# Early chunks transposed on TensorE, input loads gated behind the weights, and both matmul phases in sequence, in a retention and gated MLP kernel on one core

## The chip, the core and the metric

The kernel runs on one core of one Trainium2 chip. Times are device microseconds of that core. The kernel before took 371.13 us (median of three runs, 371.1 to 371.18). "Ratio" below always means the ratio of a kernel's fast runs to the fast runs of the kernel before in the same rounds, on the same chip ("fast": not over 1.5% above the fastest run of that kernel). It is not quite the ratio of the medians that stand beside it.

Engine names: PE is TensorE (matmul), PEld its weight load, DVE is VectorE, ACT is ScalarE, POOL is GpSimd, SP is SyncE, whose queue issues the input loads. "ACTq" and "SPq" are the issuing queues. Times inside a trace count from the start of the profiled span. PSUM is the memory that the matmuls here write to; a buffer of it can be used again only when another engine has copied the result out. A semaphore is a counter that instructions wait on; each DMA here raises one when it has completed.

## The reference

```python
# q, k, v: (8 batches, 8 heads, 576 positions, 64); float32
scores = (1/8) * q @ k.T
ret    = scores * gamma[h] ** (i - j)   for i >= j, else 0
attn   = ret @ v
x      = attn as (4608 tokens, 512)          # tokens = batch x position
h      = x @ w_in                            # 512 -> 2048
out    = (h * cos(h)) @ w_out                # 2048 -> 512, float32
```

## The kernel before

Attention works in chunks of up to 128 positions, five to a batch (128, 128, 128, 128, 64), with a running state per batch. A "full chunk" is one of 128 rows; a batch is 4.5 of them. Each chunk is loaded (q, k, v), scaled to bf16 (`qs`, `ks`, `vb`), and q and k are transposed by the DMA. The MLP works on nine tiles of 512 tokens: `mm1` gives h and g = h cos(h) for one of 16 slices of the 2048 columns, `mm2` projects back.

```python
def prep(b, c, eng_k, eng_v):                # scale to bf16, then transpose by DMA
    ...
    for dst, src in ((qT, qs), (kT, ks)):
        nc.sync.dma_start(dst[:, :, :sz], src[:sz]..., transpose=True)

def mm1(t, et):                              # h = x w_in, one of 16 slices
    ps = ps_mm.tile([P, 512], F32, tag="mm") # one of FOUR PSUM buffers, shared with mm2
    ... 4 matmuls into ps
    nc.scalar.activation(cosh, ps, Sin, bias=half_pi)
    nc.vector.tensor_mul(gT[:, et, :], ps, cosh)

def mm2(t, s):                               # o = g w_out, four matmuls a call
    ... accumulate into ps (the same four buffers)
    if qt == 3:
        nc.scalar.copy(ot, ps)               # ScalarE empties PSUM ...
        nc.scalar.dma_start(out[...], ot)    # ... and its queue issues the store

# start: loads of batch 0, preps, w_in; loads of batch 1; attention of batch 0;
# preps of batch 1, w_out, loads of batch 2; then
for t in range(NT + 1):
    for s in range(16):
        if s % 3 == 0 and s // 3 < 5:
            prep(t + 2, s // 3, ...); load(t + 3, s // 3)
        mm1(t, s); mm2(t - 1, s)             # the two phases interleaved, a tile apart
        ... one unit of the attention of batch t + 1
```

## Time and profile before

| | before |
|---|---|
| median time | 371.13 us |
| profiled span | 367.2 us |
| TensorE busy, 0 to 104 us | 47 us |
| TensorE busy, 138 to 171 us | 33 of 33 us |

The page divides the span into 40 slices (9.2 us each). A digit is the busy share in tenths, PEclk the granted TensorE clock, DMA the share of the DMA engines. Before:

```profile
PE   0013708683899999999999999999999999999995
...
PEclk9999999898799999999999999999999999999999
DMA  9999999999999999998997999721000011001012
```

TensorE works in bursts with gaps for the first eleven slices (47 of 104 us) and is full from then on. The DMA row is full for the first half. So the kernel has two stages, and only the first can be shortened without taking work from TensorE. Busy time by stretches of the span (columns: stretch, its length, then PE, PEld, DVE, ACT and POOL busy us with instruction counts, granted clock, DMA share, GB/s), before:

```profile
0.00:50.00 50.00, 11.38 (x116) 6.70 (x116) 16.05 (x35) 6.79 (x10) 17.02 (x25) 1.00 1.18 191
50.00:104.00 54.00, 35.86 (x250) 16.60 (x251) 27.83 (x39) 14.41 (x22) 27.09 (x32) 0.91 1.19 191
...
138.00:171.00 33.00, 33.00 (x239) 15.87 (x238) 21.20 (x30) 13.11 (x20) 14.80 (x17) 1.00 1.10 207
```

What TensorE waits for in the first stage, from the view of the waits (total us, times, longest), before:

```profile
PE sc L122 <- DMA kT<-ks: 55.5, 8, 20.8
```

Scores wait for the DMA transposes of k; the longest wait is 20.8 us. Two lines of TensorE's timeline (start, length, instruction, and in brackets the idle time just before and who ended it), then one of POOL's, all of the kernel before:

```profile
56.64 0.60 PE L122 MATMUL sc<-qT,kT 64*128 64x128 bf16 x8 [12.32 <-DMA kT<-ks]
...
84.48 1.03 PE L228 MATMUL o<-w_out_sb,gT 128*128 128x512 bf16 x4
```

```profile
56.85 3.04 POOL L278 DMA_DIRECT2D w_out_sb<-in_moe_w_out_dram  x4
```

w_out is issued only at 56.85 us, and the first output-projection matmul runs at 84.48 us.

### The profile page before, as it was taken

How to read it: one execution, taken by the hardware profiler on the slowest of the kernel's cores; microseconds unless marked ns; L12 is line 12 of the kernel's file. 1: busy time of each engine (PE TensorE's matmuls, PEld its weight loads, DVE VectorE, ACT ScalarE, POOL GpSimd, SP SyncE). 2: the span in 40 equal slices, each digit the busy share in tenths (PEclk: the TensorE clock that was granted, in tenths of full speed). 3: DMA queues.
4: the chain of work that ended last, by engine and by line, in shares of the span. 5: the costliest groups of instructions: out<-in, count | busy, mean ns of one | idle time of the engine just before them, and what ended most of it. 6: DMA issues, size and time to landing. Idle time of an engine off the chain costs nothing.

```text
span 367.2 us, 5413 instructions
## 1 busy us (share of the span) xinstructions
PE 306.3 (83%) x2048; PEld 145.7 (40%) x2048; DVE 187.6 (51%) x276; ACT 126.1 (34%) x189; POOL 104.9 (29%) x125
## 2 busy tenths in 40 slices
PE   0013708683899999999999999999999999999995
PEld 0002403241344444544544444445444444444442
DVE  2223605592567477556656664766576534334300
ACT  2220002242233434334334333443433354454421
POOL 3240475057544454452651524320000000000000
PEclk9999999898799999999999999999999999999999
DMA  9999999999999999998997999721000011001012
GB/s 173 209 152 199 208 202 143 198 207 202 206 180 186 213 202 206 191 231 185 192 210 167 188 203 198 172 73 43 30 29 30 30 41 46 31 37 49 30 62 81
DMA packets 161370, 51.75 MB, mean 141 GB/s; under 512 B 152640, under 2 KB 156736, under 8 KB 161344
## 3 DMA queue, kind: packets, MB, share of 16 engines
q1 hardware_dynamic: 151936, 37.77, 60.6%
q0 software_dynamic: 4224, 4.19, 7.3%
q10 hardware_dynamic: 5184, 9.44, 7.3%
q8 instruction: 16, 0.26, 0.3%
q14 instruction: 10, 0.08, 0.1%
HBM read 36.70 MB, written 9.44 MB: 126 GB/s over the span
## 4 chain that ended last, share of the span: by engine, by line
PE 72%; DMA 13%; SPq 11%; POOL 2%; issue 1%; DVE 1%; ACT 0%; POOLq 0%
PE o L228 32%; PE h L209 31%; SPq L88 8%; DMA kT<-ks 7%; DMA fq<-in_q_dram 3%; DMA fv<-in_v_dram 3%; PE sc L122 3%; PE ov L179 3%; SPq L110 2%; PE st L144 1%; PE ov L169 1%; POOL qs L101 1%; POOL vb L106 1%; DVE ret L130 0%; ACT cosh L217 0%
## 5 line engine op out<-in xcount | busy, mean ns | idle before, releaser
L217 ACT ACTIVATE cosh<-h,half_pi 128x512 f32<-128x512 f32 x144 | 98.8, 687 | 205.2 <-PE h L209 203.0
L218 DVE TENSOR_TENSOR gT<-h,cosh 128x512 bf16<-128x512 f32 x144 | 99.5, 691 | 113.8 <-ACT cosh L217 113.1
L209 PE MATMUL h<-xT,w_in_sb 128*128 128x512 bf16 x576 | 152.8, 389 | 0.0
L228 PE MATMUL o<-w_out_sb,gT 128*128 128x512 bf16 x576 | 145.5, 380 | 0.0
L228 PEld LDWEIGHTS <-gT 128*128 128x128 bf16 x576 | 56.5, 98 | 68.4 <-issue 0.8
L209 PEld LDWEIGHTS <-w_in_sb 128*128 128x128 bf16 x576 | 50.1, 99 | 52.8 <-issue 3.8
L101 POOL TENSOR_TENSOR qs<-fq,gq 128x512 bf16<-128x512 f32 (+1 forms) x40 | 41.7, 1042 | 77.9 <-DMA fq<-in_q_dram 77.5
L122 PE MATMUL sc<-qT,kT 64*128 64x128 bf16 (+1 forms) x320 | 16.8, 231 | 55.6 <-DMA kT<-ks 55.5
L130 DVE TENSOR_TENSOR ret<-sc,tri 128x1024 bf16<-128x1024 f32 (+1 forms) x40 | 44.3, 1108 | 32.0 <-PE sc L122 31.9
L102 POOL TENSOR_TENSOR ks<-fk,gk 128x512 bf16<-128x512 f32 (+1 forms) x35 | 36.5, 1042 | 23.6 <-DMA kT<-ks 16.6
L122 PEld LDWEIGHTS <-kT 64*128 64x128 bf16 (+1 forms) x320 | 9.7, 103 | 72.5 <-DMA kT<-ks 59.6
L106 POOL CAST vb<-fv 128x512 bf16<-128x512 f32 (+1 forms) x35 | 21.3, 610 | 41.9 <-PE ov L179 34.9
L237 ACT COPY ot<-o 128x512 f32<-128x512 f32 x36 | 21.1, 586 | 17.1 <-PE o L228 16.9
L188 DVE CAST xT<-ov 128x512 bf16<-128x512 f32 (+1 forms) x40 | 25.3, 633 | 1.3 <-PE ov L179 0.8
L153 DVE TENSOR_TENSOR sb<-st,diag_104 128x512 bf16<-128x512 f32 x32 | 21.8, 681 | 0.0
L179 PE MATMUL ov<-ret,vb 128*64 128x128 bf16 (+1 forms) x320 | 17.0, 232 | 0.0
L169 PE MATMUL ov<-qT,sb 128*128 128x128 bf16 (+1 forms) x128 | 12.5, 225 | 1.4 <-DVE xT L188 1.4
L144 PE MATMUL st<-vb,ks 128*128 128x128 bf16 x128 | 13.5, 233 | 0.0
L169 PEld LDWEIGHTS <-sb 128*128 128x128 bf16 x128 | 9.8, 103 | 9.1 <-issue 2.8
L144 PEld LDWEIGHTS <-ks 128*128 128x128 bf16 x128 | 10.2, 104 | 7.7 <-issue 1.5
L179 PEld LDWEIGHTS <-vb 128*64 128x64 bf16 (+1 forms) x320 | 10.5, 116 | 6.5 <-issue 3.9
L102 DVE TENSOR_TENSOR ks<-fk,gk 128x512 bf16<-128x512 f32 (+1 forms) x5 | 3.6, 715 | 14.3 <-DMA fk<-in_k_dram 14.3
(22 smaller groups left out, 14.7 us busy)
## 6 DMA issues: line engine op xcount, KB each, us to landing
out_dram<-ot ACTq DMA_DIRECT2D x36, 256.0 KB, 2.1
fq<-in_q_dram SPq DMA_DIRECT2D x32, 256.0 KB, 4.3
fk<-in_k_dram SPq DMA_DIRECT2D x32, 256.0 KB, 4.6
fv<-in_v_dram SPq DMA_DIRECT2D x32, 256.0 KB, 5.1
w_in_sb<-in_moe_w_in_dram POOLq DMA_DIRECT2D x4, 512.0 KB, 10.5
w_out_sb<-in_moe_w_out_dram POOLq DMA_DIRECT2D x4, 512.0 KB, 10.8
fq<-in_q_dram SPq DMA_DIRECT2D x8, 128.0 KB, 3.9
fk<-in_k_dram SPq DMA_DIRECT2D x8, 128.0 KB, 4.5
```

The costliest lines, as they stand in the source:

```text
L88: nc.sync.dma_start(f[:sz], src[b, :, c * P : c * P + sz, :].rearrange("h s d -> s h d"))
L101: nc.gpsimd.tensor_tensor(out=qs[:sz], in0=fq[:sz], in1=tq, op=ALU.mult)
L102: eng_k.tensor_tensor(out=ks[:sz], in0=fk[:sz], in1=tk, op=ALU.mult)
L122: nc.tensor.matmul(ps[:sz, he, hg, :sz], lhsT=kT[d0 : d0 + D, hg, :sz], rhs=qT[d0 : d0 + D, hg, :sz], start=True, stop=True,)
L130: nc.vector.tensor_tensor(out=ret[:sz, :, :, :sz].rearrange("p a b i -> p (a b) i"), in0=ps[:sz, :, :, :sz].rearrange("p a b i -> p (a b) i"),
L144: nc.tensor.matmul(ps[:, hg, :], lhsT=ks[:, 2 * hg : 2 * hg + 2, :].rearrange("s h d -> s (h d)"), rhs=vb[:, 2 * hg : 2 * hg + 2, :].rearr ...
L169: nc.tensor.matmul(ps[:, hg, :sz], lhsT=sb[:, hg, :], rhs=qT[:, hg, :sz], start=(hg == 0), stop=False, skip_group_check=True,)
L179: nc.tensor.matmul(ps[he * D : he * D + D, hg, :sz], lhsT=vb[:sz, 2 * hg + he, :], rhs=ret[:sz, he, hg, :sz], start=(c == 0 and hg == 0), ...
L209: nc.tensor.matmul(ps, lhsT=w_in_sb[:, dg, et * P : (et + 1) * P], rhs=xT[:, dg, t0 : t0 + T_TILE], start=(dg == 0), stop=(dg == DG - 1),)
L217: nc.scalar.activation(cosh, ps, ACTF.Sin, bias=half_pi, scale=1.0)
L218: nc.vector.tensor_mul(gT[:, et, :], ps, cosh)
L228: nc.tensor.matmul(ps, lhsT=gT[:, et, tsi * P : (tsi + 1) * P], rhs=w_out_sb[:, et, :], start=(et == 0), stop=(et == ET - 1),)
```

## The change

The intent is to make the start short. Chunks 0 to 7 are transposed on TensorE instead of by DMA. Loads of chunks 4, 5 and 6 (and, as the queue is in order, all later ones) wait until parts of w_out have landed. The first tiles have 512, 256 and 256 tokens, so that less attention has to be ready for tiles 1 and 2. Each tile does all of mm1, then all of mm2, with the attention of the next tile between the mm2 matmuls. In tile 0 the mm2 of its four 128-token groups advances side by side; later tiles finish one `o` after the other. The core of the diff (cuts marked):

```diff
+    widths = [512, 256, 256] + [512] * 7
+    N_PE_T = 8
+    AHEAD = 6
+    LEAD = 4
+    GATED = {4: 4, 5: 6, 6: 7}
-    op = ctx.enter_context(tc.tile_pool(name="op", bufs=3))
+    op = ctx.enter_context(tc.tile_pool(name="op", bufs=4))
 ...
+        if g >= N_PE_T:
+            for m in range(2):
+                nc.sync.dma_start(qkT[:, m, :, :sz], ..., transpose=True)
 ...
+    def transposes(g):                        # chunks 0..7
+        ps = ps_ov.tile([P, 2, HG, P], BF16, tag="ov", name="tr")
+        ... 8 x nc.tensor.transpose(ps[...], qks[...], ident)
+        nc.vector.tensor_copy(qkT[:, :, :, :sz], ps[:, :, :, :sz])
+
+    def scores(g):
+        if g >= 4:
+            feed(g + 1 + LEAD)                # loads up to AHEAD chunks further, then preps
 ...
+    for g in range(4):
+        prep(g, nc.vector, nc.scalar)
+        if g == 2: load_w_in(0, 256); load_w_in(256, 512)
+    ... rest of w_in, then w_out in four parts
+    for u in units(0, 4): u()
 ...
+    for n, w in enumerate(widths):
+        for et in range(ET):
+            mm1(n, et)
+        ...
+        for i, group in enumerate(groups):    # groups of four mm2 matmuls
+            for tsi, et in group:
+                mm2(n, tsi, et)               # ends, as before, with nc.scalar.copy(ot, ps)
+                                              # and nc.scalar.dma_start(out[...], ot)
+            ... the next tile's attention units, spread over the groups
```

More of the change, by code (lines that the diff above doesn't have):

```diff
@@ L44 @@
     gammas = [1.0 - 2.0 ** (-5.0 - h) for h in range(H)]
-    T_TILE = 512
-    NT = NTOK // T_TILE
     DG = DM // P
     ET = DF // P
-    NQ = T_TILE // P
+    widths = [512, 256, 256] + [512] * 7
+    assert sum(widths) == NTOK
+    starts = [sum(widths[:n]) for n in range(len(widths))]
+    chunks = [(b, c) for b in range(B) for c in range(NC)]
+    N_PE_T = 8
+    AHEAD = 6
+    LEAD = 4
+    GATED = {4: 4, 5: 6, 6: 7}
     consts = ctx.enter_context(tc.tile_pool(name="consts", bufs=1))
@@ L64 @@
     ps_mm = ctx.enter_context(tc.tile_pool(name="ps_mm", bufs=4, space=bass.MemoryType.PSUM))
-    order = ctx.enter_context(tc.manual_schedule())
+    ctx.enter_context(tc.manual_schedule())
     pos_i = consts.tile([P, NC, H], I32)
@@ L77 @@
     diag2 = consts.tile([P, P], F32)
+    ident = consts.tile([P, P], BF16)
     w_in_sb = consts.tile([P, DG, DF], BF16)
@@ L82, with load, prep @@
     tiles = {}
-    def load(b, c):
+    def load(g):
+        b, c = chunks[g]
         sz = csz[c]
+        first = None
         for name, src in (("q", q), ("k", k), ("v", v)):
             f = ld.tile([P, H, D], F32, tag="f" + name, name=f"f{name}")
-            nc.sync.dma_start(
+            i = nc.sync.dma_start(
                 f[:sz], src[b, :, c * P : c * P + sz, :].rearrange("h s d -> s h d")
             )
-            tiles["f" + name, b, c] = f
-    def prep(b, c, eng_k, eng_v):
+            first = first or i
+            tiles["f" + name, g] = f
+        return first
+    def prep(g, eng_k, eng_v):
+        b, c = chunks[g]
         sz = csz[c]
-        fq, fk, fv = (tiles.pop(("f" + n, b, c)) for n in "qkv")
-        qs = nat.tile([P, H, D], BF16, tag="qs", name="qs")
-        ks = nat.tile([P, H, D], BF16, tag="ks", name="ks")
+        fq, fk, fv = (tiles.pop(("f" + n, g)) for n in "qkv")
+        qks = nat.tile([P, 2, H, D], BF16, tag="qks", name="qks")
         vb = nat.tile([P, H, D], BF16, tag="vb", name="vb")
@@ L100, in prep @@
         tk = gk[:sz, c, :].unsqueeze(2).to_broadcast([sz, H, D])
-        nc.gpsimd.tensor_tensor(out=qs[:sz], in0=fq[:sz], in1=tq, op=ALU.mult)
-        eng_k.tensor_tensor(out=ks[:sz], in0=fk[:sz], in1=tk, op=ALU.mult)
+        nc.gpsimd.tensor_tensor(out=qks[:sz, 0], in0=fq[:sz], in1=tq, op=ALU.mult)
+        eng_k.tensor_tensor(out=qks[:sz, 1], in0=fk[:sz], in1=tk, op=ALU.mult)
         if eng_v is nc.scalar:
@@ L106, in prep @@
             eng_v.tensor_copy(vb[:sz], fv[:sz])
-        kT = trp.tile([P, HG, P], BF16, tag="kT", name="kT")
-        qT = trp.tile([P, HG, P], BF16, tag="qT", name="qT")
-        for dst, src in ((qT, qs), (kT, ks)):
-            nc.sync.dma_start(
-                dst[:, :, :sz], src[:sz].rearrange("s h d -> s (h d)"), transpose=True
-            )
-        tiles["a", b, c] = (ks, vb, qT, kT)
-    def scores(b, c):
-        sz = csz[c]
-        ks, vb, qT, kT = tiles["a", b, c]
+        qkT = trp.tile([P, 2, HG, P], BF16, tag="qkT", name="qkT")
+        if g >= N_PE_T:
+            for m in range(2):
+                nc.sync.dma_start(
+                    qkT[:, m, :, :sz],
+                    qks[:sz, m].rearrange("s h d -> s (h d)"),
+                    transpose=True,
+                )
+        tiles["a", g] = (qks, vb, qkT)
+    def transposes(g):
+        sz = csz[chunks[g][1]]
+        qks, vb, qkT = tiles["a", g]
+        ps = ps_ov.tile([P, 2, HG, P], BF16, tag="ov", name="tr")
+        for m in range(2):
+            for hg in range(HG):
+                nc.tensor.transpose(
+                    ps[:, m, hg, :sz],
+                    qks[:sz, m, 2 * hg : 2 * hg + 2, :].rearrange("s h d -> s (h d)"),
+                    ident[:sz, :sz],
+                )
+        nc.vector.tensor_copy(qkT[:, :, :, :sz], ps[:, :, :, :sz])
+    def scores(g):
+        if g >= 4:
+            feed(g + 1 + LEAD)
+        sz = csz[chunks[g][1]]
+        qks, vb, qkT = tiles["a", g]
         ps = ps_sc.tile([P, 2, HG, P], F32, tag="sc", name="sc")
@@ L123, in scores @@
                     ps[:sz, he, hg, :sz],
-                    lhsT=kT[d0 : d0 + D, hg, :sz],
-                    rhs=qT[d0 : d0 + D, hg, :sz],
+                    lhsT=qkT[d0 : d0 + D, 1, hg, :sz],
+                    rhs=qkT[d0 : d0 + D, 0, hg, :sz],
                     start=True,
@@ L135, in scores, with state @@
         )
-        tiles["ret", b, c] = ret
-    def state(b, c):
-        ks, vb, qT, kT = tiles["a", b, c]
+        tiles["ret", g] = ret
+    def state(g):
+        b, c = chunks[g]
+        qks, vb, qkT = tiles["a", g]
         if c == 0:
@@ L145, in state @@
                 ps[:, hg, :],
-                lhsT=ks[:, 2 * hg : 2 * hg + 2, :].rearrange("s h d -> s (h d)"),
+                lhsT=qks[:, 1, 2 * hg : 2 * hg + 2, :].rearrange("s h d -> s (h d)"),
                 rhs=vb[:, 2 * hg : 2 * hg + 2, :].rearrange("s h d -> s (h d)"),
@@ L158, in state, with attn_out @@
         )
-        tiles["sb", b, c + 1] = sb
-    def attn_out(b, c):
+        tiles["sb", g + 1] = sb
+    def attn_out(g):
+        b, c = chunks[g]
         sz = csz[c]
-        ks, vb, qT, kT = tiles.pop(("a", b, c))
-        ret = tiles.pop(("ret", b, c))
+        qks, vb, qkT = tiles.pop(("a", g))
+        ret = tiles.pop(("ret", g))
         ps = ps_ov.tile([P, HG, P], F32, tag="ov", name="ov")
         if c > 0:
-            sb = tiles.pop(("sb", b, c))
+            sb = tiles.pop(("sb", g))
             for hg in range(HG):
@@ L171, in attn_out @@
                     lhsT=sb[:, hg, :],
-                    rhs=qT[:, hg, :sz],
+                    rhs=qkT[:, 0, hg, :sz],
                     start=(hg == 0),
@@ L188, in attn_out, with units, mm1 @@
         nc.vector.tensor_copy(xT[:, :, t0 : t0 + sz], ps[:, :, :sz])
-    def attention_units(b):
-        u = [
-            lambda: scores(b, 0), lambda: state(b, 0), lambda: scores(b, 1),
-            lambda: attn_out(b, 0), lambda: state(b, 1), lambda: scores(b, 2),
-            lambda: attn_out(b, 1), lambda: state(b, 2), lambda: scores(b, 3),
-            lambda: attn_out(b, 2), lambda: state(b, 3), lambda: scores(b, 4),
-            lambda: attn_out(b, 3), lambda: attn_out(b, 4),
-        ]
-        return u
-    def mm1(t, et):
-        t0 = t * T_TILE
+    def units(g0, g1):
+        u = []
+        if g0 < min(g1, N_PE_T):
+            u.append(lambda g=g0: transposes(g))
+        for g in range(g0, g1):
+            if g + 1 < min(g1, N_PE_T):
+                u.append(lambda g=g + 1: transposes(g))
+            u.append(lambda g=g: scores(g))
+            if g > g0:
+                u.append(lambda g=g - 1: attn_out(g))
+            if chunks[g][1] < NC - 1:
+                u.append(lambda g=g: state(g))
+        if g1 > g0:
+            u.append(lambda g=g1 - 1: attn_out(g))
+        return u
+    def mm1(n, et):
+        t0, w = starts[n], widths[n]
         if et == 0:
-            tiles["g", t] = gp.tile([P, ET, T_TILE], BF16, tag="gT", name="gT")
-        gT = tiles["g", t]
-        ps = ps_mm.tile([P, T_TILE], F32, tag="mm", name="h")
+            tiles["g", n] = gp.tile([P, ET, 512], BF16, tag="gT", name="gT")
+        gT = tiles["g", n]
+        ps = ps_mm.tile([P, 512], F32, tag="mm", name="h")
         for dg in range(DG):
             nc.tensor.matmul(
-                ps,
+                ps[:, :w],
                 lhsT=w_in_sb[:, dg, et * P : (et + 1) * P],
-                rhs=xT[:, dg, t0 : t0 + T_TILE],
+                rhs=xT[:, dg, t0 : t0 + w],
                 start=(dg == 0),
@@ L215, in mm1, with mm2 @@
             )
-        cosh = cosp.tile([P, T_TILE], F32, tag="cosh", name="cosh")
-        nc.scalar.activation(cosh, ps, ACTF.Sin, bias=half_pi, scale=1.0)
-        nc.vector.tensor_mul(gT[:, et, :], ps, cosh)
-    def mm2(t, s):
-        gT = tiles["g", t]
-        tsi, qt = divmod(s, 4)
-        if qt == 0:
-            tiles["o", t] = ps_mm.tile([P, DM], F32, tag="mm", name="o")
-        ps = tiles["o", t]
-        for et in range(qt * 4, qt * 4 + 4):
-            nc.tensor.matmul(
-                ps,
-                lhsT=gT[:, et, tsi * P : (tsi + 1) * P],
-                rhs=w_out_sb[:, et, :],
-                start=(et == 0),
-                stop=(et == ET - 1),
-            )
-        if qt == 3:
+        cosh = cosp.tile([P, 512], F32, tag="cosh", name="cosh")
+        nc.scalar.activation(cosh[:, :w], ps[:, :w], ACTF.Sin, bias=half_pi, scale=1.0)
+        nc.vector.tensor_mul(gT[:, et, :w], ps[:, :w], cosh[:, :w])
+    def mm2(n, tsi, et):
+        gT = tiles["g", n]
+        if et == 0:
+            tiles["o", n, tsi] = ps_mm.tile([P, DM], F32, tag="mm", name="o")
+        ps = tiles["o", n, tsi]
+        nc.tensor.matmul(
+            ps,
+            lhsT=gT[:, et, tsi * P : (tsi + 1) * P],
+            rhs=w_out_sb[:, et, :],
+            start=(et == 0),
+            stop=(et == ET - 1),
+        )
+        if et == ET - 1:
             ot = op.tile([P, DM], F32, tag="o", name="ot")
             nc.scalar.copy(ot, ps)
-            t0 = t * T_TILE + tsi * P
+            t0 = starts[n] + tsi * P
             nc.scalar.dma_start(out[t0 : t0 + P, :], ot)
-    for c in range(NC):
-        load(0, c)
+    for g in range(4):
+        load(g)
     nc.gpsimd.iota(pos_i, pattern=[[P, NC], [0, H]], base=-MID, channel_multiplier=1)
@@ L247 @@
         tri, tri, pattern=[[1, P]], compare_op=ALU.is_ge, fill=0.0, base=0, channel_multiplier=-1
+    )
+    nc.gpsimd.affine_select(
+        ident, tri, pattern=[[-1, P]], compare_op=ALU.is_ge, fill=0.0, base=0, channel_multiplier=1
     )
@@ L261 @@
     nc.scalar.activation(gk, pos, ACTF.Exp, bias=0.0, scale=-1.0)
-    for c in range(NC):
-        prep(0, c, nc.vector, nc.scalar)
-    WCH = 512
-    for e0 in range(0, DF, WCH):
-        nc.gpsimd.dma_start(
-            w_in_sb[:, :, e0 : e0 + WCH],
-            moe_w_in[:, e0 : e0 + WCH].rearrange("(dg p) e -> p dg e", p=P),
-        )
-    for c in range(NC):
-        load(1, c)
-    for u in attention_units(0):
-        u()
-    for c in range(NC):
-        prep(1, c, nc.gpsimd, nc.gpsimd)
@@ L277 @@
-    for g0 in range(0, ET, 4):
-        nc.gpsimd.dma_start(
-            w_out_sb[:, g0 : g0 + 4, :],
-            moe_w_out[g0 * P : (g0 + 4) * P, :].rearrange("(eg p) c -> p eg c", p=P),
-        )
-    for c in range(NC):
-        load(2, c)
-    for t in range(NT + 1):
-        units = attention_units(t + 1) if t + 1 < B else []
-        for s in range(ET):
-            if s % 3 == 0 and s // 3 < NC:
-                c = s // 3
-                if t + 2 < B:
-                    prep(t + 2, c, nc.gpsimd, nc.gpsimd)
-                if t + 3 < B:
-                    load(t + 3, c)
-            if t < NT:
-                mm1(t, s)
-            if t >= 1:
-                mm2(t - 1, s)
-            if s < len(units):
-                units[s]()
+    w_dma = []
@@ new lines, in load_w_in, with load_w_out @@
+    def load_w_in(e0, e1):
+        w_dma.append(nc.gpsimd.dma_start(
+            w_in_sb[:, :, e0:e1], moe_w_in[:, e0:e1].rearrange("(dg p) e -> p dg e", p=P)
+        ))
+    def load_w_out(g0, g1):
+        w_dma.append(nc.gpsimd.dma_start(
+            w_out_sb[:, g0:g1, :],
+            moe_w_out[g0 * P : g1 * P, :].rearrange("(eg p) c -> p eg c", p=P),
+        ))
+    for g in range(4):
+        prep(g, nc.vector, nc.scalar)
+        if g == 2:
+            load_w_in(0, 256)
+            load_w_in(256, 512)
@@ new lines, with gate, feed @@
+    load_w_in(512, 1024)
+    load_w_in(1024, 2048)
+    for g0 in range(0, ET, 4):
+        load_w_out(g0, g0 + 4)
+    for u in units(0, 4):
+        u()
+    def gate(ins, w):
+        tc.add_manual_dep(
+            ins.ins, w.ins.name,
+            mybir.DependencyInfo(mybir.DependencyClass.Sync, mybir.DependencyReason.DATA),
+            reason="weights first",
+        )
+    loaded, prepared = 4, 4
+    def feed(n):
+        nonlocal loaded, prepared
+        while loaded < len(chunks) and (loaded < n + AHEAD or prepared < n):
+            i = load(loaded)
+            if loaded in GATED:
+                gate(i, w_dma[GATED[loaded]])
+            loaded += 1
+            if prepared < n and prepared + AHEAD < loaded:
+                prep(prepared, nc.gpsimd, nc.gpsimd)
+                prepared += 1
+        while prepared < min(n, len(chunks)):
+            prep(prepared, nc.gpsimd, nc.gpsimd)
+            prepared += 1
@@ new lines @@
+    feed(4 + LEAD)
+    done = 4
+    for n, w in enumerate(widths):
+        for et in range(ET):
+            mm1(n, et)
+        need = done
+        if n + 1 < len(widths):
+            end = starts[n + 1] + widths[n + 1]
+            while need < len(chunks) and chunks[need][0] * S + chunks[need][1] * P < end:
+                need += 1
+        todo = units(done, need)
+        total = len(todo)
+        done = need
+        nts = w // P
+        if n == 0:
+            mms = [(tsi, et) for et in range(ET) for tsi in range(nts)]
+        else:
+            mms = [(tsi, et) for tsi in range(nts) for et in range(ET)]
+        groups = [mms[i : i + 4] for i in range(0, len(mms), 4)]
+        for i, group in enumerate(groups):
+            for tsi, et in group:
+                mm2(n, tsi, et)
+            want = -(-total * (i + 1) // max(1, len(groups) - 2))
+            while todo and total - len(todo) < want:
+                todo.pop(0)()
```

## The prediction

> **What bounds the kernel now.** Two stages (busy time by windows). From about 104 us TensorE is 100% busy at granted clock 1.00. A 512-token tile takes 33.5 us there (timeline, 206.0 to 239.6): 32 groups of four 512-column matmuls at 0.863 us are 27.6 us, one batch of attention (4.5 full chunks) is 5.9 us. Before 104 us TensorE has only 48 us of busy time and waits for DMA: by the waits, scores wait for kT transposes, up to 20.8 us in one wait. The timeline of the SP queue shows why: inputs of three batches (13.5 full chunks) and their DMA transposes go out before or beside w_out, which is issued only at 56.9 us; the first output-projection matmul starts at 84.3 us. The chain of waits agrees: PE 72%, DMA 13%, SP queue 11%.
>
> **What changes, with costs.**
> - Chunks 0-7 get 8 TensorE transposes and one PSUM copy each. A load without competition took 3.6 us a chunk; two DMA transposes take 2.5 us of SP issue, up to 6 under load. TensorE pays about 0.5 us a chunk (four 128-column matmuls take 0.2-0.3 us warm), VectorE about 1.1 us. The Trainium skill, "TensorE: Matmul & The Clock Gate", Part 4, names ~275 ns for one 128x128 transpose in a kernel and the PSUM copy after it: 2.2 us a chunk, still in time in which TensorE waits. No trace here shows it yet.
> - Loads of chunks 4, 5, 6 wait for w_out parts, so the weights get the DMA engines alone. Their queue's share was 7.3% of 367 us: 27 us.
> - mm1 then mm2 of the same tile: no extra TensorE work. In mm1 a PSUM buffer is held about 2.7 us (0.86 + 0.69 + 0.69 + hand-over) against 3.45 us for four, so no steady stall.
>
> **Ledger (estimate from these durations).** Chunks 0-3 land at 17.4 us, w_in is issued from 12.5 us; mm1 of tile 0 starts near 24 us instead of 42.4. All weights are in at 2.8 + 4x3.6 + 27 = 44 us. Chunks 5, 6 land at 46-50 us; as TensorE is in order, it waits 6-8 us inside mm2 of tile 0. Tile 1 starts near 63 us. The new weak spot: the queue issues loads six chunks ahead of the DMA transposes, so chunk 8's transposes leave SP only at about 76 us, and chunk 12's, needed for tile 3, land at 2.8 + 17.5x3.6 + 27 + 4.5x2.5 = 104 us. Tile 3 starts near 107 us. From there TensorE is full: seven tiles x 27.6 + 5.4 batches of attention x 5.9 = 225 us, plus 4 us tail and 1-2 us at half clock after the waits: span 338 us. Before, at that moment, 257 us were left. The time runs 2-4 us over the span (371.13 against 367.2).
>
> **Prediction: 340 us, 331 to 351 with 8 chances in 10.** Faster by over 2%: 0.95; within 2%: 0.04; slower: 0.01.
>
> **What would show the steps right.** First h matmul at 22-28 us; first o matmul near 40; w_out landed by 42-50; TensorE waits on DMA of chunks 5-6 (fq, fk) around 42-53 us and on kT of chunks 8-12 around 76-107; full slices after about 107; steady tiles still 33-34 us; ACT and VectorE never hold TensorE for long in mm1.
>
> **What would make it wrong.** Weights alone slower than 27 us (all shifts up to 12 us), or faster; transposes landing so late behind the loads ahead of them that tile 4 waits too; the 256-token tiles bound by ScalarE and PSUM buffers (1-3 us); half-clock TensorE after each wait; stalls at phase borders, where the last xT copy must land before the next mm1: 1 us each would add 9 us.

## The result, and the profile after

The changed kernel takes 357.75 us (median of four runs, 357.32 to 358.3); before took 371.12 us in the same rounds. The ratio is 0.9644 (95% interval 0.9627 to 0.9661): faster by 3.6%. The predicted range was 331 to 351 us, so the direction was right and the size was not.

The same rows of the page, after (8.9 us to a slice), with the ACT row added:

```profile
PE   1078999203999999999999999999999999999995
...
ACT  2123700002708057107513831471175118414721
...
PEclk9989999855799999999999999999999999999999
DMA  9999999999967997899679809961610310011011
```

TensorE starts much earlier and is full in slices 5 to 7. Then comes a hole that the kernel before doesn't have: slice 9 shows TensorE and ScalarE at 0 together, with TensorE at 2 and 3 on either side, while the DMA row stays at 9. (ScalarE is also at 0 in slices 6 and 7, but there TensorE runs mm2, which needs it only at the end.) The same in stretches of the span:

```profile
0.00:31.00 31.00, 11.36 (x127) 8.15 (x128) 16.01 (x35) 5.49 (x8) 11.38 (x20) 0.94 1.17 199
31.00:64.00 33.00, 32.28 (x216) 15.31 (x215) 19.19 (x27) 11.58 (x17) 18.64 (x21) 1.00 1.17 197
64.00:90.00 26.00, 3.76 (x18) 2.10 (x18) 0.69 (x2) 2.95 (x7) 9.97 (x11) 0.60 1.03 206
90.00:127.00 37.00, 35.10 (x320) 23.10 (x319) 26.76 (x49) 14.35 (x33) 13.43 (x16) 0.96 0.92 185
127.00:160.00 33.00, 33.00 (x239) 15.88 (x238) 22.38 (x30) 13.32 (x20) 13.54 (x17) 1.00 0.99 190
```

From 64 to 90 us TensorE worked 3.76 of 26 us, at a granted clock of 0.60. From 127 us on everything is as full as before. The Trainium skill, page "TensorE: Matmul & The Clock Gate", section "What's actually happening", says that TensorE falls to half clock after about 3.4 us of idling and needs about as long of work to come back; this trace agrees roughly. In windows of 1 us the granted clock is 1.00 up to 69 us, 4.5 us after the last matmul (64.5 us), and 0.50 from there on; it is back at 1.00 in the window from 93 us, some 3 us after TensorE runs without gaps again (89.8 us). At 0.50 four 256-column matmuls take 1.01 us instead of 0.6.

The waits, after:

```profile
ACT ot L271 <- PE o L262: 150.3, 33, 18.1
...
PE h L246 <- ACT ot L271: 21.8, 3, 18.2
ACT ot L271 <- DMA qkT<-qks: 18.2, 1, 18.2
```

The first line is harmless: ScalarE is not the bottleneck. The second is the hole. `PE h` is the first matmul phase of tile 1, and it waits for `ot`, the copy with which ScalarE empties the output PSUM of tile 0. The third says what `ot` itself waited for: a DMA transpose. The copy reads only PSUM and writes an `ot` buffer that nobody had used yet, so it has no business with a transpose. (In the kernel before, the same line of the waits, `ACT ot` on a DMA transpose, has 0.2 us in all, and `ACT cosh` on one 1.4 us.) ScalarE's own timeline shows what happened:

```profile
63.27 0.58 ACT L271 COPY ot<-o 128x512 f32<-128x512 f32 x1 [18.08 <-PE o L262]
81.67 0.38 ACTq L273 DMA_DIRECT2D out_dram<-ot  x1
82.09 0.58 ACT L271 COPY ot<-o 128x512 f32<-128x512 f32 x1 [18.23 <-DMA qkT<-qks]
84.44 0.34 ACTq L273 DMA_DIRECT2D out_dram<-ot  x1
84.82 0.58 ACT L271 COPY ot<-o 128x512 f32<-128x512 f32 x1 [2.14 <-DMA fq<-in_q_dram]
87.22 0.40 ACTq L273 DMA_DIRECT2D out_dram<-ot  x1
```

ScalarE copies the first o tile at 63.27 us. Its next instruction in order is the issue of that tile's store (ACTq, 273). It starts at 81.67 us. Then copy and issue alternate. The second and third issue are held up again, by 1.8 us each; the fourth, at 88.36 us, follows its copy (87.65 to 88.23 us) almost at once. TensorE's timeline in the same time:

```profile
61.12 2.76 PE L262 MATMUL o<-w_out_sb,gT 128*128 128x512 bf16 x12
63.91 0.60 PE L246 MATMUL h<-xT,w_in_sb 128*128 128x256 bf16 x4
82.73 1.01 PE L246 MATMUL h<-xT,w_in_sb 128*128 128x256 bf16 x4 [18.22 <-ACT ot L271]
85.45 1.01 PE L246 MATMUL h<-xT,w_in_sb 128*128 128x256 bf16 x4 [1.71 <-ACT ot L271]
88.29 1.01 PE L246 MATMUL h<-xT,w_in_sb 128*128 128x256 bf16 x4 [1.82 <-ACT ot L271]
...
127.01 4.26 PE L246 MATMUL h<-xT,w_in_sb 128*128 128x512 bf16 x19
```

Tile 1's first h group gets a PSUM buffer at 63.91 us. The next three need the buffers of the other three o tiles and wait 18.2, 1.7 and 1.8 us for ScalarE. The last line is tile 3's first matmul, at 127.01 us.

What did the store wait for? A listing of the instructions with the semaphores that each waits for (the built program, not the profile; row, source line, instruction; PE, DVE, Pool and Activation are the engines' own semaphores) has ScalarE's queue at this point:

```
11 L271 TensorCopy ot<-o 128x512 [waits PE_49]
12 L273 DMACopy out_dram<-ot 128x512 [waits DMAHW2_49,Activation_49]
13 L271 TensorCopy ot<-o 128x512 [waits PE_49]
14 L273 DMACopy out_dram<-ot 128x512 [waits DMAHW4_49,Activation_49]
15 L271 TensorCopy ot<-o 128x512 [waits PE_49]
16 L273 DMACopy out_dram<-ot 128x512 [waits DMAHW6_49,Activation_49]
17 L271 TensorCopy ot<-o 128x512 [waits PE_49]
18 L273 DMACopy out_dram<-ot 128x512 [waits DMAHW7_49,Activation_49]
```

and SP's queue:

```
51 L123 DmaTransposeAnt qkT<-qks 128x4x64 [waits DMAHW2_49,DVE_49,Pool_49]
52 L123 DmaTransposeAnt qkT<-qks 128x4x64 [waits DMAHW3_49,Pool_49]
53 L98 DMACopy fq<-in_q_dram 128x8x64 [waits DMAHW4_49]
54 L98 DMACopy fk<-in_k_dram 128x8x64 [waits DMAHW5_49]
55 L98 DMACopy fv<-in_v_dram 128x8x64 [waits DMAHW6_49,Pool_49]
56 L123 DmaTransposeAnt qkT<-qks 128x4x128 [waits DMAHW7_49,DVE_49,Pool_49]
57 L123 DmaTransposeAnt qkT<-qks 128x4x128 [waits DMAHW0_49,Pool_49]
58 L98 DMACopy fq<-in_q_dram 128x8x64 [waits DMAHW1_49]
59 L98 DMACopy fk<-in_k_dram 128x8x64 [waits DMAHW3_49]
```

The DMAs that SP and ACT issue take eight completion semaphores (DMAHW0 to 7) in turn, in program order over both queues, and each waits until the last user of its semaphore has completed. Between rows 58 (semaphore 1) and 59 (semaphore 3) the first store took semaphore 2, whose last user is row 51, chunk 9's q transpose. Stores two to four follow rows 53, 55 and 56: a load of q and of v for chunk 16, and a transpose of chunk 10. A rebuild of the program gave the same semaphores, and wait values that are the completion counts of just these DMAs. SP's timeline shows when they went out:

```profile
77.45 3.45 SPq L123 DMA_TRANSPOSE qkT<-qks  x2
80.95 0.57 SPq L98 DMA_DIRECT2D fq<-in_q_dram  x1
...
82.24 1.12 SPq L98 DMA_DIRECT2D fv<-in_v_dram  x1
83.47 3.77 SPq L123 DMA_TRANSPOSE qkT<-qks  x2
```

Chunk 9's transposes (77.45) come just before the first store at 81.67 us, chunk 16's q (80.95) before the second at 84.44, its v (82.24) before the third at 87.22, chunk 10's transposes (83.47) before the fourth, which hardly waited. The Trainium skill, page "DMA: Bandwidth & Descriptors", section "Why a DMA increments its semaphore by 16 and not by 1", warns that two DMAs in flight on one semaphore can let a wait pass too early, and asks for "One semaphore per in-flight slot". No run here shows such an early pass: in the listing every DMA waits for the earlier user of its semaphore. The waits above are what safe reuse of eight of them costs when one queue is far behind.

So the theory: a store on ScalarE's queue stands behind a DMA that program order put far back in SP's queue, ScalarE is in order and stops, PSUM stays full (all four buffers, by tile 0's order of mm2), TensorE stops. Two rivals: the data that TensorE needs next (chunks 7 to 12, their transposes) is late anyway, and the wait only shows where it starts; or stores collide with the DMA traffic itself.

### The profile page after: what moved, and what is told of

Read it like the earlier page. It is cut to its first block, busy times and chain, and to the rows that moved or that the text cites. A ratio compares the mean times of both kernels' runs of the same rounds, so it can differ in the third digit from the quotient of the medians.

```text
span 356.2 us, 5733 instructions
## 1 busy us (share of the span) xinstructions
PE 307.8 (86%) x2176; PEld 155.3 (44%) x2176; DVE 200.1 (56%) x299; ACT 128.1 (36%) x204; POOL 105.6 (30%) x128
## 4 chain that ended last, share of the span: by engine, by line
PE 80%; DMA 7%; SPq 5%; DVE 4%; issue 1%; ACT 1%; POOL 1%; ACTq 0%; POOLq 0%
PE o L262 35%; PE h L246 35%; SPq L98 4%; PE ov L211 3%; PE sc L152 3%; DMA fk<-in_k_dram 3%; DMA qkT<-qks 2%; PE ov L201 2%; PE st L175 2%; DMA fv<-in_v_dram 2%; SPq L123 1%; DVE ret L160 1%; PE tr L136 1%; DVE qkT L141 1%; DVE xT L220 1%
## 5 line engine op out<-in xcount | busy, mean ns | idle before, releaser
L246 PE MATMUL h<-xT,w_in_sb 128*128 128x512 bf16 (+1 forms) x640 | 129.7, 364 | 23.4 <-ACT ot L271 21.8
L255 DVE TENSOR_TENSOR gT<-h,cosh 128x512 bf16<-128x512 f32 (+1 forms) x160 | 101.5, 638 | 76.7 <-ACT cosh L254 76.3
L254 ACT ACTIVATE cosh<-h,half_pi 128x512 f32<-128x512 f32 (+1 forms) x160 | 101.5, 644 | 35.6 <-PE h L246 34.5
L246 PEld LDWEIGHTS <-w_in_sb 128*128 128x128 bf16 x640 | 63.8, 100 | 88.0 <-issue 24.8
L114 POOL TENSOR_TENSOR qks<-fq,gq 128x512 bf16<-128x512 f32 (+1 forms) x40 | 41.6, 1040 | 42.1 <-DMA fq<-in_q_dram 30.0
L115 POOL TENSOR_TENSOR qks<-fk,gk 128x512 bf16<-128x512 f32 (+1 forms) x36 | 37.4, 1040 | 1.3 <-DMA fk<-in_k_dram 1.2
L136 PE MATMUL tr<-ident,qks 128*128 128x128 bf16 (+1 forms) x64 | 6.1, 249 | 17.2 <-DVE qkT L141 10.7
L152 PE MATMUL sc<-qkT 64*128 64x128 bf16 (+1 forms) x320 | 15.8, 221 | 1.6 <-DVE qkT L141 0.8
L152 PEld LDWEIGHTS <-qkT 64*128 64x128 bf16 (+1 forms) x320 | 9.3, 99 | 16.5 <-issue 14.5
L175 PE MATMUL st<-vb,qks 128*128 128x128 bf16 x128 | 12.9, 225 | 0.0
L201 PE MATMUL ov<-qkT,sb 128*128 128x128 bf16 (+1 forms) x128 | 11.9, 218 | 1.0 <-DVE xT L220 0.6
```

Of the source, the lines that this page charges most:

```text
L114: nc.gpsimd.tensor_tensor(out=qks[:sz, 0], in0=fq[:sz], in1=tq, op=ALU.mult)
L115: eng_k.tensor_tensor(out=qks[:sz, 1], in0=fk[:sz], in1=tk, op=ALU.mult)
L152: nc.tensor.matmul(ps[:sz, he, hg, :sz], lhsT=qkT[d0 : d0 + D, 1, hg, :sz], rhs=qkT[d0 : d0 + D, 0, hg, :sz], start=True, stop=True,)
L201: nc.tensor.matmul(ps[:, hg, :sz], lhsT=sb[:, hg, :], rhs=qkT[:, 0, hg, :sz], start=(hg == 0), stop=False, skip_group_check=True,)
L246: nc.tensor.matmul(ps[:, :w], lhsT=w_in_sb[:, dg, et * P : (et + 1) * P], rhs=xT[:, dg, t0 : t0 + w], start=(dg == 0), stop=(dg == DG - 1),)
L254: nc.scalar.activation(cosh[:, :w], ps[:, :w], ACTF.Sin, bias=half_pi, scale=1.0)
```

## The experiments

All give correct results. All runs are fast, but for two of the four of e7_pool_no_pe_t; e12_sp_stores did not build. Times are medians of four runs.

| run | edit against the changed kernel | us | ratio to before |
|---|---|---|---|
| (changed kernel) | | 357.75 | 0.9644 |
| e1_pool_stores | stores issued by POOL | 342.38 | 0.9242 |
| e2_pool_tile0 | only tile 0's stores by POOL | 350.38 | 0.9477 |
| e3_ahead1 | loads 1 chunk ahead of the transposes, not 6 | 341.14 | 0.9212 |
| e13_sp_stores6 | stores issued by SP, six `ot` buffers | 340.53 | 0.9167 |
| e4_no_pe_t | no transposes on TensorE | 361.0 | 0.9782 |
| e7_pool_no_pe_t | e1 and no transposes on TensorE | 362.26 (its two fast runs: 359.5) | 0.9676 |
| e5_pool_no_gate | e1 and no gating | 342.54 | 0.9228 |
| e6_pool_w512 | e1 and nine tiles of 512 | 349.87 | 0.9416 |
| e8_pool_ahead1 | e1 and e3 | 336.81 | 0.9071 |
| e9_start_only | start in another order | 356.7 | 0.9645 |
| e10_pool_ahead1_start | e8 and e9 | 331.91 | 0.8976 |
| e11_pool_pe13_start | e1, e9, and 13 chunks transposed on TensorE | 335.13 | 0.9064 |

### Stores by POOL

```diff
-            nc.scalar.dma_start(out[t0 : t0 + P, :], ot)
+            nc.gpsimd.dma_start(out[t0 : t0 + P, :], ot)
```

> All output stores are issued from the POOL queue instead of the ACT queue. Theory (completion semaphores): in the changed kernel the first store of tile 0 waits on the ACT queue from 63.9 to 81.7 us for the completion of a DMA that is far back in the SP queue, because stores on ACT and loads on SP take turns on the same eight completion semaphores; ACT then can't drain PSUM. Then the 18.2 + 1.8 + 1.7 us waits of the h matmuls for the ot copies vanish, h of tile 1 runs on from 64 us, and the time is 333 to 341 us. Rival (data): chunks 7 to 12 and their DMA transposes are not there in time anyway, TensorE only waits elsewhere: the time stays within 352 to 358 us, with the waits moved to the scores.

Measured: 342.38 us, ratio 0.9242 (0.9202 to 0.9282), about 1 us above the expected range and far from the rival's 352 to 358. The clock may have a part in that: in the profiled run (342.58 us) the granted clock was 0.50 from 26 to 34 us and the h matmuls of tile 0 took 15.77 us, against 13.97 us in the changed kernel. ScalarE's timeline in e1:

```profile
65.42 2.05 ACT L271 COPY ot<-o 128x512 f32<-128x512 f32 x4 [18.08 <-PE o L262]
67.33 6.93 ACT L254 ACTIVATE cosh<-h,half_pi 128x256 f32<-128x256 f32 x16
```

The four copies now run in a row (2.05 us for four), and the cosines follow. TensorE's timeline in e1:

```profile
68.35 5.40 PE L246 MATMUL h<-xT,w_in_sb 128*128 128x256 bf16 x48 [0.23 <-DVE gT L255]
...
102.82 0.61 PE L152 MATMUL sc<-qkT 64*128 64x128 bf16 x8 [4.54 <-DMA qkT<-qks]
...
109.68 13.98 PE L246 MATMUL h<-xT,w_in_sb 128*128 128x512 bf16 x64
```

The h matmuls of tile 1 run on at 68 us. One wait for data is left: 4.54 us before the scores of the last chunk that tile 3 needs, at 102.82 us. Tile 3 starts at 109.68 us instead of 127.01. So the rival "data is late anyway" is worth some 4.5 us of the 21.8, not all of it. That wait is the weak spot that the prediction had named. In the listing of e1 the stores have eight other semaphores (DMASW0 to 7), which only POOL's DMAs use; the first eight of them follow the loads of the weights.

### Only tile 0's stores by POOL

```diff
-            nc.scalar.dma_start(out[t0 : t0 + P, :], ot)
+            (nc.gpsimd if n == 0 else nc.scalar).dma_start(out[t0 : t0 + P, :], ot)
```

> Only the four stores of tile 0 go over the POOL queue; the others stay on ACT. Semaphore theory: the wait moves to the first store of tile 1, whose predecessor on its semaphore stands still farther back in the SP queue (a transpose of chunk 11 or a load of chunk 17, done near 90 us): a wait of about 10 us on ACT, time 341 to 350 us, between e1 and the changed kernel. Rival (only the first stores are special, or data): the same as e1, or no change.

Measured: 350.38 us, 0.4 us above the range that the theory gave, and clearly between e1 and the changed kernel. The wait moved to tile 1's two stores (issued at 90.86 and 97.88 us). ScalarE's waits in e2:

```profile
ACT ot L271 <- DMA fq<-in_q_dram: 11.8, 1, 11.8
ACT cosh L254 <- DMA fk<-in_k_dram: 6.4, 1, 6.4
```

These are the DMAs that the semaphores name: in a listing of e2's program, the two stores wait for the load of q of chunk 17 and of k of chunk 18. There is nothing special about the first store: whichever store comes while SP's queue is far ahead in program order pays.

### Loads one chunk ahead

```diff
-    AHEAD = 6
+    AHEAD = 1
```

> Loads are put on the SP queue one chunk ahead of the DMA transposes instead of six; stores stay on ACT. Semaphore theory: the DMA that the first store waits for stands nearer to the front of the SP queue (load of chunk 10, done near 65 us), so the waits of ACT at 64 to 88 us shrink to about 6 us in all: 337 to 345 us. Rival (the stores collide with DMA traffic, whatever the order): no change, 355 to 360 us.

Measured: 341.14 us, as expected. Stores are still on ScalarE; only the order of SP's queue changed, so that the DMAs that the stores follow are done sooner. TensorE's waits in e3:

```profile
PE h L246 <- ACT ot L271: 4.8, 3, 4.0
```

4.8 us are left of 21.8, the longest where the second store follows a load of k (4.0 us on ScalarE), as the listing of e3 has it. A collision with traffic whatever the order would have left the time as it was. The rival "data is late" isn't set apart by e3 alone, as the transposes too come earlier; e1, e2 and e13 do that.

### Stores by SP

```diff
-    op = ctx.enter_context(tc.tile_pool(name="op", bufs=4))
+    op = ctx.enter_context(tc.tile_pool(name="op", bufs=6))
-            nc.scalar.dma_start(out[t0 : t0 + P, :], ot)
+            nc.sync.dma_start(out[t0 : t0 + P, :], ot)
```

A first form with eight buffers (e12_sp_stores) did not build: 16 KB a partition were wanted and 13.875 KB left.

> As e12, which had no room for eight ot buffers, with six: stores on the SP queue. They share hardware queue and semaphores with the loads, and leave later than in e1 (behind the loads of chunk 17, past 85 us), but ACT doesn't wait for them at tile 0. If a blocked ACT is what holds TensorE, and not a late or colliding store: no wait of h for ot at 64 us, 338 to 348 us. If late stores as such hurt: 355 us or more.

Measured: 340.53 us, ratio 0.9167 (0.9133 to 0.92). SP's and TensorE's timelines in e13:

```profile
86.60 1.99 SPq L273 DMA_DIRECT2D out_dram<-ot  x4
```

```profile
66.55 5.40 PE L246 MATMUL h<-xT,w_in_sb 128*128 128x256 bf16 x48 [0.23 <-DVE gT L255]
```

The four stores of tile 0 go out in one row from 86.60 us, about as late as in the changed kernel (81.7 to 88.4), on the loads' own queue and semaphores. Tile 1's h matmuls run at 66.55 us all the same. So a late store cost nothing here, nor did a store beside loads; ScalarE stopped at the issue was the cost. (The six buffers are a second change; e1 had its gain with four. That e13 is 0.8% below e1 is not read as a merit of SP: h of tile 0 took 13.97 us in e13's trace and 15.77 us in e1's.)

### No transposes on TensorE

```diff
-    N_PE_T = 8
+    N_PE_T = 0
```

> Undo: no chunk is transposed on TensorE; all go by DMA transposes as before, the rest of the change stays. If the early TensorE transposes are what makes the start fast, chunk 0 to 3's transposes leave SP at 14 to 26 us and those of chunks 4 to 7 only behind the loads of chunks 10 to 13, past 60 us, so TensorE waits inside mm2 of tile 0 and the stores wait longer: 362 to 378 us. If they are worth little: within 2 per cent of 357.8 us.

Measured: 361.0 us, ratio 0.9782, only 1.4% over the changed kernel (0.9782/0.9644) and just below the range; against the kernel before the record calls it unclear at 2%. One of its four runs took 365.0 us; the others lie within 360.5 to 361.2. Read alone, this undo says that the transposes on TensorE bring little. In e4 TensorE waits for DMA transposes instead and starts h late; its waits and its first h matmuls:

```profile
PE sc L152 <- DMA qkT<-qks: 44.9, 6, 21.9
```

```profile
48.53 16.08 PE L246 MATMUL h<-xT,w_in_sb 128*128 128x512 bf16 x64 [0.79 <-DVE xT L220]
```

48.53 us instead of 30.50. But TensorE, coming later, finds the stores released. ScalarE's timeline in e4:

```profile
89.56 0.58 ACT L271 COPY ot<-o 128x512 f32<-128x512 f32 x1 [24.23 <-PE o L262]
90.18 0.37 ACTq L273 DMA_DIRECT2D out_dram<-ot  x1
```

The first store is issued right behind its copy, at 90.18 us, and so are the other three of tile 0; the 18.2 us are gone. One wait hides the other. So the undo was repeated with the store wait removed (e1 with N_PE_T = 0):

> Stores on POOL, and no transposes on TensorE. In e4 (stores on ACT) this undo cost only 3 us, as it also shortened the wait of the stores. Without that wait the early TensorE transposes should show what they are worth: 352 to 359 us, 10 to 17 us over e1. If they are worth as little as e4 says: 343 to 347 us.

Measured: 362.26 us (two runs near 359.5 us counted fast, two near 365 us counted slow; both pairs have the clocks 0.981 and 0.989, so the clock does not explain the step, and its cause stays open); the ratio of the fast runs, 0.9676, is 4.7% over e1 (0.9676/0.9242), some 16 us, at the upper end of the range. That is what the early transposes are worth with loads six chunks ahead; no run tried this undo with one chunk ahead. The same undo showed a third of it in e4.

### No gating

```diff
-    GATED = {4: 4, 5: 6, 6: 7}
+    GATED = {}
```

(with stores by POOL)

> Stores on POOL (as e1, 342.4 us), and no load waits for the weights. If gating matters by itself: the weights share the DMA engines with the loads of chunks 4 to 10 from 13 us on, w_out is complete only past 60 us instead of 41 us, and the time is over 350 us. If only the sum of the DMA work up to chunk 12's transposes counts (the ledger of the prediction), tile 3 starts at 108 to 114 us as in e1 (109.7 us) and the time is 341 to 348 us.

Measured: 342.54 us, ratio 0.9228 against e1's 0.9242: the same. Gating alone is worth nothing here that these runs can tell. Tile 3 starts at 107.7 us (109.7 in e1). This fits the expectation that only the sum of the DMA's work up to chunk 12's transposes counts, which is the same in either order; that this is the reason is argued, not shown.

### Nine tiles of 512

```diff
-    widths = [512, 256, 256] + [512] * 7
+    widths = [512] * 9
```

(with stores by POOL)

> Stores on POOL, and nine tiles of 512 tokens. Tile 1 then needs chunk 8, whose DMA transposes leave SP only near 74 us, so TensorE waits some 13 us inside mm2 of tile 0; part of it comes back, as chunk 12 is waited for less. Tokens from 1024 on start near 115 us instead of 109.7 us: 345 to 352 us. If the two tiles of 256 bring nothing: 340 to 344 us.

Measured: 349.87 us, as expected; 1.9% over e1 (0.9416/0.9242). TensorE gets one wait for chunk 8's transposes, 13.9 us, of which some 7 us show in the time, in part because e1's wait for chunk 12 (4.5 us) is gone:

```profile
PE sc L152 <- DMA qkT<-qks: 13.9, 1, 13.9
```

### Both mends, and the start

e8 joins e1 and e3 (POOL stores, AHEAD = 1):

> Stores on POOL and loads one chunk ahead of the transposes. Both waits that are left in e1 (4.5 us for chunk 12's transposes) and in e3 (about 6 us of ACT) should be gone, tile 3 starts near 104 us: 333 to 338 us. If e1 and e3 took the same time from the same place and the rest is TensorE work: 339 to 342 us.

Measured: 336.81 us, ratio 0.9071. TensorE's row of the page in e8 has no hole after slice 3:

```profile
PE   1078999998989999999999999999999999999992
```

What is left to gain lies before 31 us. VectorE's timeline of the changed kernel shows why TensorE starts that late:

```profile
16.12 0.69 DVE L115 TENSOR_TENSOR qks<-fk,gk 128x512 bf16<-128x512 f32 x1 [2.80 <-DMA fk<-in_k_dram]
16.73 0.68 DVE L141 COPY qkT<-tr 128x1024 bf16<-128x1024 bf16 x1
```

VectorE scales k of chunk 3 (L115) when it has landed, and only then copies chunk 0's transposes out of PSUM (L141, 16.73 us), which have lain there since about 6.8 us: the program emits all four preps before the first attention unit, and VectorE is in order. The edit emits each chunk's attention units before the next chunk's prep:

```diff
+    todo0, done_u = units(0, 4), 0
+    g4 = ["t0", "t1", "s0", "st0", "t2", "s1", "o0", "st1", "t3", "s2", "o1", "st2", "s3", "o2", "st3", "o3"]
     for g in range(4):
         prep(g, nc.vector, nc.scalar)
         if g == 2:
             load_w_in(0, 256)
             load_w_in(256, 512)
+        first = g4.index(f"t{g + 1}") if g < 3 else len(g4)
+        while done_u < first:
+            todo0[done_u]()
+            done_u += 1
 ...
-    for u in units(0, 4):
-        u()
```

First alone, on the changed kernel:

> Only the order of the start is changed against the changed kernel (stores stay on ACT): the attention work of chunk 0, 1, 2 is put before the preparation of the next chunk in program order, so that VectorE copies chunk 0's transposes near 6.5 us instead of 16.7 us, and h of tile 0 starts near 24 us instead of 30.5 us. If the wait of the stores for the SP queue bounds tile 1 (its end is set by DMA, 81.7 us), TensorE only arrives earlier and waits longer: 355 to 359 us, the same. If an earlier start is worth what it saves: 350 to 353 us.

Measured: 356.7 us, ratio 0.9645 against 0.9644: nothing, although h starts at 25.51 us instead of 30.50. TensorE's timeline and waits in e9:

```profile
25.51 15.45 PE L246 MATMUL h<-xT,w_in_sb 128*128 128x512 bf16 x64 [0.79 <-DVE xT L220]
```

```profile
PE h L246 <- ACT ot L271: 23.7, 3, 20.2
```

The wait for `ot` is 23.7 us instead of 21.8, and tile 1 still resumes at 82.6 us. That moment is set by SP's queue, so TensorE only arrives earlier (tile 1's first group at 61.81 us instead of 63.91; h of tile 0 took 15.45 us instead of 13.97) and waits longer. Then together with e8:

> The same start with stores on POOL and loads one chunk ahead (e8, 336.8 us, where TensorE hardly waits after 31 us). Now the start should count: h of tile 0 near 24 us. TensorE then meets chunks 4 to 6, gated behind w_out, some 3 us too early, so 329 to 334 us. If the start doesn't count here either: 336 to 338 us.

Measured: 331.91 us, ratio 0.8976 (0.8947 to 0.9005), 1.0% under e8 (0.8976/0.9071). The same edit that was worth nothing is worth 3 to 5 us once the wait behind it is gone. The page of e10:

```profile
PE   1689989999999999999999999999999999999992
...
PEclk9999999999999999999999999999999999999999
```

TensorE is at 8 or more from slice 3 and full from slice 7 to the one before the last. The clock row shows 9 throughout, but the durations contradict it at the start: the h matmuls of tile 0 took 15.69 us here and 13.97 us in the changed kernel, and four transposes take 0.61 us at 17.62 us and 0.39 us at 46.45 us. So TensorE ran slower until about 29 us, and the row does not show it. This is the fastest version tried, and TensorE's own work is most of what is left in it (308.8 us busy in a span of 329.7).

Last, six loads ahead as in the change, but no tile up to tile 3 in need of a DMA transpose (N_PE_T = 13):

> The same start, stores on POOL, loads six ahead as in the change, but thirteen chunks transposed on TensorE, so that tiles 0 to 3 need no DMA transpose. If the late transposes of chunks 8 to 12 are all that is wrong with six loads ahead: 330 to 335 us, near e10; the five further chunks cost TensorE about 2.5 us and some waits for the PSUM copies. If six ahead hurts later tiles as well: over 337 us.

Measured: 335.13 us, 1.0% over e10 (0.9064/0.8976), 0.1 us above the range. So six loads ahead can be kept if the early chunks don't need the SP queue, but the extra transposes and the waits for their PSUM copies cost more than a shorter look-ahead: TensorE is busy for 311.4 us against 308.8, and tile 3 starts at 102.4 us against 98.5.

## Why the prediction was wrong, point by point

- **What bounds the kernel before: right.** The first stage was DMA, the second TensorE; steady tiles take 33.5 us in both kernels (206.0 to 239.6 us before; 127.0 to 160.6 us after).
- **"mm1 then mm2 of the same tile: no extra TensorE work ... so no steady stall": right in the steady stage.** From 127 us the changed kernel needs 229.2 us to its end; the ledger said 225 + 4.
- **"ACT and VectorE never hold TensorE for long in mm1": this step failed.** The ledger counted ScalarE's busy time and PSUM's hold time, and took the store's issue for free. ScalarE's queue was held for 18.2 us, then 2.1 and 2.2 us, by the semaphore of DMAs far back in SP's queue; TensorE lost 21.8 us to it directly, and ran at half clock (0.50) after it. The prediction had named the back of the SP queue as "the new weak spot", but only for the transposes behind it, not for a store on another engine. With that wait removed (e1) tile 3 starts at 109.7 us against the ledger's 107, and with another look-ahead (e3) at 109.7 too, instead of 127.0; the times, 342.4 and 341.1 us, are in the predicted range of 331 to 351 us. e2, e3 and e13 show that it is the wait at the issue, not the store or its traffic.
- **"Tile 1 starts near 63 us": right** (63.9 us), but by luck: two misses cancel. **"mm1 of tile 0 starts near 24 us": wrong**, 30.5 us, outside the 22 to 28 us given. The ledger missed that VectorE, in order, holds chunk 0's PSUM copy behind chunk 3's k (10.7 us). **"It waits 6-8 us inside mm2 of tile 0": wrong**, there was no such wait. The weights were in at about 41 us instead of 44 (chunk 6's load, gated behind the last part of w_out, is issued at 40.81 us). That TensorE came later is not the whole reason: in e10, where it starts at 25.2 us, the longest wait for a chunk in mm2 of tile 0 is 0.4 us.
- **Chunk 12's transposes at 104 us: right where it can be seen.** In e1 the scores that wait for them run at 102.8 us. In the changed kernel they leave SP from 95.4 to 98.6 us, so they were not what held tile 3 until 127.0 us.
- **TensorE transposes: the cost was right where TensorE runs at full clock, 0.45 us for eight (47.49 to 47.94 us in the trace); at the start eight took twice that, 0.95 us (17.46 to 18.41 us).** The Trainium skill, "TensorE: Matmul & The Clock Gate", section "Part 4: PE-mode transpose", names about 275 ns for one; the trace's median for one is 219 ns, but eight in a row overlap; eight times the page's figure, 2.2 us as an estimate, would have been far too much. **The PSUM copy was over-estimated**: 0.68 us for 1024 bf16 columns against 1.1. The skill's page "VectorE: DVE Perf Modes", section "Why PSUM operands drop a tier", would have told it: PSUM caps at double rate for 16-bit data and at single rate for fp32. The trace agrees: 1024 bf16 columns take as long as 512 fp32 columns (0.68 us each).
- **Gating: not needed for the ledger.** The prediction let the weights have the DMA alone; e5 shows the same time without that. Its ledger had added up the DMA's work, and that sum held. The order of loads and transposes does move the time (e8 against e1, 1.8%).

What stays open: no run separates the half clock after the hole from the hole itself. An estimate from the trace bounds it: three groups of 1.01 us instead of 0.60 and 48 matmuls of 6.91 us instead of 5.40 make at most 2.7 of the 16 us between e1 and the changed kernel. That the store and the transpose share a semaphore is read from the listing and from the matching times of three stores; e1, where the stores have other semaphores, and the DMAs that e2 and e3 wait for bear it out, but no run changed the semaphores alone, with the stores left on ScalarE. Nor did one finish tile 0's `o` one after the other, so that fewer PSUM buffers hang on the first store.

## What to carry to other kernels

An issue of a DMA was here an instruction of an in-order queue that could wait: for its data, and for the earlier user of its completion semaphore, which could belong to another queue. So don't let the engine that empties PSUM issue stores while another queue has been filled far ahead in program order; let an engine with slack issue them, or keep the look-ahead short. And judge one part of a change only after the wait that hides it is gone: the same undo measured 1.4% and 4.7%, the same improvement of the start 0 and 1.0%.

## What the Trainium skill lacked or had wrong

- "DMA: Bandwidth & Descriptors", section "Issuing engines are not separate DMA queues", says that issuing from several engines only saves the sequencer's time, which is usually small. Here the choice of the issuing engine for 36 stores moved the time from a ratio of 0.9644 to 0.9242 (e1), as the issuing queue also waits for semaphores; the page doesn't mention that an issue can block its engine's compute (18.2 us here). The page "Perfetto Trace Analysis", section "DMA Instruction — HWDGE (DVE, Sync)", does draw the wait for semaphores as a stage of the issuing sequencer; it gives it no cost either.
- The same page, "Why a DMA increments its semaphore by 16 and not by 1": it asks for one semaphore per slot in flight, but says nothing of what waiting for a shared one costs; 21.8 us of TensorE here.
- "TensorE: Matmul & The Clock Gate", "Part 4: PE-mode transpose": it gives the length of one, about 275 ns, but not the pace of several in a row (the page has one for plain matmuls, in Part 1). Eight in a row took 0.45 us to the next instruction here, 56 ns each, and that is the figure to plan with.
